# Attention beside a gated feature layer on one core: feature tiles end in pairs, row maxima go bank by bank, and the eight PSUM banks are named by hand

## The chip, the cores and the metric

The kernel runs on one core of a Trainium2 chip. The metric is the device time of one execution in microseconds. The core has five engines with a queue of instructions each: TensorE (PE in the profile, its weight loads PEld), VectorE (DVE), ScalarE (ACT), GpSimd (POOL) and SyncE (SP, which here only issues DMAs). Each queue runs in order; across queues, instructions wait for one another through semaphores. TensorE writes its results to PSUM, which this kernel uses as eight banks of 128 x 512 fp32 values.

## The reference

For one sequence x of S = 2048 tokens and D = 448 features:

```
g   = sigmoid(x . gate_w)                                   one number a token
a   = (softmax(q k^T / sqrt(28)) v) wo                      16 heads of 28 features
b   = (relu(x W_gate) * (x W_up)) W_down                    1792 hidden features
out = g * a + (1 - g) * b
```

All data are fp32. TensorE gets fp32 precision from reduced-precision passes by splitting operands into a high and a low part: a product over the 448 features takes eleven passes (the list TERMS), since the last 64 features of both parts share one pass with another.

## The kernel before, in words

The order of the instructions is written out by hand; no scheduler moves them. The work has three stages.

*The front part* projects x to q, k and v. Units of eleven passes for q and k (`qk`, line 324) alternate with units for v (`vproj`, line 342). From the tenth unit on, row maxima of the first heads and, at the end, the first 16 scores are put between the passes.

*The rounds* are the bulk: 256 pairs of head and key tile (16 heads, 16 tiles of 128 keys), eight tiles a round, 32 rounds. Each character of an order string is one step:

- `s` is one block of scores, 128 keys by 512 queries (`scores`, line 180, TensorE), and its exponential (line 182, ScalarE) into a slot for probabilities. Four blocks make a key tile, 32 a round.
- `m` is a piece of the row maxima that softmax subtracts (`smax`). For 128 queries, TensorE computes the products with the keys (line 152) and VectorE takes the largest (line 154). A head needs 16 x 4 blocks of 128 x 512. Maxima run ahead of the scores by LEAD tiles and more. When a head is finished, `smax_end` transposes its 128 x 16 maxima (line 162), splits them and writes them by DMA as two extra rows of Q, so that the score matmul subtracts them.
- `x` is one pass of the feature layer of b (`gu_mm`, line 489): a half tile is 128 of the gate or of the up features for 512 tokens and takes eleven passes. A finished gate half goes through relu (`relu`, ScalarE, in LATE rounds VectorE), a finished up half is multiplied by it on VectorE and sent to DRAM (`spill_h`, lines 505 and 511).
- `h` ends two half tiles together: their last passes need only 64 rows each, sit in the upper and the lower half of the array, and run side by side. This is called a pair here.
- `l` and `u` are steps of the first round alone: the last store of the front part, and the loads of the third head with the split of the second half of the first weights.

After the string of a round come the splits of the next feature weights (`split_f`: ScalarE the high part, POOL the low part, line 99), then `pv` (line 524): the value product of the eight key tiles, 32 fp32 matmuls, which the trace records as 64, on column tiles of 32, into one bank. It goes to OS by a copy on ScalarE (line 528, first half of a head) or an add on VectorE (line 530, second half).

`FIRST` is the order of the first round, `LONG` has three half tiles in a round, `WIDE` four, and `LATE` is for the last three rounds, which have no maxima.

PSUM comes from three pools of the scheduling layer: `ps_s`, two banks for scores; `ps_x`, two for feature passes and the transpose; `ps_w`, two tiles of two banks each for maxima and value products. The layer chooses which buffer of a pool a new tile gets.

*The rest* after the rounds has five feature tiles (`gate_up`), the down projection (line 741), the output projection (`wout`, line 697) and the mix of both.

The small steps that the prediction speaks of: `row_sums` (line 538) inverts the sums of the probabilities of a head, `spread` broadcasts them by DMA from POOL's queue, `normalise` (line 549) multiplies. SP's queue carries the loads of K and Q of later heads (lines 134 and 139) and of the raw feature weights (`fetch_f`, line 209), in the order in which they are issued. The raw weights of the first tile lie in a buffer called `pair`, whose other half holds the last stored qk tile until its DMA is done; the third Q takes that buffer.

Of the kernel before, what the change touches and what calls it, by code (L numbers as in the profile page):

```python
# [29 lines left out]
NK = S // P  # L30
SCALE = DH ** -0.5
# [36 lines left out]
def gated_mix_kernel(ctx, tc, x, wq, wo, wgu, wd, out):  # L68
# [11 lines left out]
    def ps_s(name):  # L80
        return psum.tile([P, TB], F32, tag="s", bufs=2, name=name)

    def ps_w(name):
        return psum.tile([P, 2, TB], F32, tag="mx", bufs=2, name=name)

    def ps_x(name):
        return psum.tile([P, TB], F32, tag="x", bufs=2, name=name)
# [54 lines left out]
    maxima = [(h, u, half) for h in range(H) for u in range(NK) for half in range(2)]  # L142

    def smax(k):

        h, u, half = maxima[k]
        if u == 0 and half == 0:
            MX[h] = keep.tile([P, 32], F32, name=f"mx_{h}", tag="mx", bufs=2)
        ps = ps_w(f"sm_{k}")
        for c in range(2):  # L150
            k0 = (half * 2 + c) * TB
            nc.tensor.matmul(ps[:, c, :], Q[h][:GD, u * P:(u + 1) * P], K[h % 3][:GD, k0:k0 + TB],  # L152
                             start=True, stop=True)
        nc.vector.tensor_reduce(MX[h][:, 2 * u + half:2 * u + half + 1], ps, axis=AX.XY, op=OP.max)  # L154
        if u == NK - 1 and half == 1:
            M[h] = keep.tile([P, 16], F32, name=f"m_{h}", tag="m", bufs=2)
            nc.vector.tensor_reduce(M[h], MX.pop(h).rearrange("p (a b) -> p a b", b=2), axis=AX.X, op=OP.max)

    def smax_end(h):

        pt = ps_x(f"mt_{h}")
        nc.tensor.transpose(pt[:16, :P], M.pop(h), ident)  # L162
        mh = keep.tile([16, 2, P], F32R, name=f"mh_{h}", tag="mh", bufs=1)
# [7 lines left out]
        return rest  # L171
# [3 lines left out]
    def scores(i, j):  # L175
        h, kt = divmod(i, NK)
        if j == 0:
            PT[i] = p_slot(i % NP, f"P_{i}")
        ps = ps_s(f"s_{i}_{j}")
        nc.tensor.matmul(ps, K[h % 3][:GD + 2, kt * P:(kt + 1) * P], Q[h][:GD + 2, j * TB:(j + 1) * TB],  # L180
                         start=True, stop=True)
        nc.scalar.activation(PT[i][:, j], ps, AF.Exp, scale=SCALE)  # L182

    def scores_pair(i, j):

        h, kt = divmod(i, NK)
        if j == 0:
            PT[i] = p_slot(i % NP, f"P_{i}")
        ps = ps_w(f"s_{i}_{j}")
        for c in range(2):  # L190
            nc.tensor.matmul(ps[:, c], K[h % 3][:GD + 2, kt * P:(kt + 1) * P], Q[h][:GD + 2, (j + c) * TB:(j + c + 1) * TB],  # L191
                             start=True, stop=True)
        nc.scalar.activation(PT[i][:, j:j + 2], ps, AF.Exp, scale=SCALE)
# [18 lines left out]
    with tc.tile_pool(name="qkv", bufs=1) as pa:  # L212
# [82 lines left out]
        turn = [3]  # L295

        def ps_any(name, late=False):
            turn[0] += 1
            return (ps_s, ps_s, ps_x, ps_x)[turn[0] % 4](name) if not late else ps_x(name)
# [21 lines left out]
        def qk(tb, c, terms=TERMS, among=()):  # L321
            ps = ps_any(f"qk_{tb}_{c}", c == NQ - 1)
# [12 lines left out]
            sends.append(send)  # L335
            if (tb, c) != (0, NQ - 1):
                sends.pop()()

        def vproj(tb, t, among=()):
            ps = ps_any(f"v_{tb}_{t}", tb == 0 and t > 1)  # L340
# [26 lines left out]
        ps = ps_x("warm_ps")  # L367
# [49 lines left out]
        m, first, ahead = 0, 9, 2 * LEAD + 4  # L417
        for n, (f, *a) in enumerate(mixed):
# [16 lines left out]
            while n >= first and m < (n + 1 - first) * ahead / (len(mixed) - first):  # L435
                among.append((smax, m))
                m += 1
# [5 lines left out]
            if 0 in M and ends >= 2 * NK:  # L443
                smax_end(0)()
        assert m == ahead, m

    def gates():
# [11 lines left out]
    SECOND = {sum(n for _, n in ROUNDS[:r + 1]) - 1 - 2 * k for r in range(len(ROUNDS))  # L459
              for k in range(ROUNDS[r][0].count("h"))}  # L460
# [53 lines left out]
    NI = H * NK  # L514
    OS, LS = {}, {}

    def pv(i0, ni):

        h = i0 // NK
        po = ps_w(f"po_{i0}")[:, 0]  # L520
# [5 lines left out]
        if i0 % NK == 0:  # L526
            OS[h] = fe.tile([P, TB], F32, name=f"os_{h}", tag="os", bufs=2)
            nc.scalar.activation(OS[h], po, AF.Copy)
        else:
            nc.vector.tensor_tensor(OS[h], po, OS[h], op=OP.add)  # L530
# [62 lines left out]
    wor = None  # L593
    for r, (order, nu) in enumerate(ROUNDS):
# [5 lines left out]
        rest = None  # L600
        if m % (2 * NK) == 0 and i0 <= NI - LEAD:
            rest = smax_end(m // (2 * NK) - 1)
            if late:
                rest()
# [6 lines left out]
        for o in order:  # L611
            if o == "x" and not passes:
                continue
            if o == "s":
                i, j = i0 + 1 + ns // NB, ns % NB
                if ns == 4 * NB:
                    small_things(i0 // 4 + 1)
                if len(EARLY) <= i * NB + j < NI * NB and not late:
                    scores(i, j)
                elif late and i < NI and j % 2 == 0:  # L620
                    scores_pair(i, j)
                ns += 1
            elif o == "m":
                smax(m)
                m += 1

                if rest:
                    rest()
                    rest = None
            elif o == "x":  # L630
                i, half, n = passes.pop(0)
                if n == 0:
                    ps = (ps_s if late and len(units) < 2 else ps_x)(f"gu_{i}_{half}")
                    units.append((i, half, ps))
                gu_mm(units[-1][2], i, half, n)
                if n == NT - 1:
                    i, half, ps = units.pop()
                    spill_h(i, ps) if half else relu(i, ps, late)
# [32 lines left out]
    assert i0 == NI and m == len(maxima), (i0, m)  # L671
# [19 lines left out]

    def wout(tb, t):
        if t % 2 == 0:
            GA[tb, t // 2] = ps_w(f"wo_{tb}_{t}")
        ps = GA[tb, t // 2]
        for n, (a, b) in enumerate(TERMS):
            nc.tensor.matmul(ps[:, t % 2, :D], ON[tb][b // 4][:, b % 4, t * P:(t + 1) * P], WO[:, a], start=(n == 0),  # L697
# [3 lines left out]
        if t % 2:  # L701
            for u in (t - 1, t):
                k = tb * 4 + u
                nc.vector.tensor_scalar(GA[tb][:, u], ps[:, u % 2, :D], gate[:, 0, k:k + 1], None, op0=OP.mult)

    def gate_up(i):
# [8 lines left out]
        relu(i, ps[:, 0])  # L715
        spill_h(i, ps[:, 1])
# [37 lines left out]
    def down(i):  # L754
        tb, f = divmod(i, NF)
        if f == 0:
            ACC[tb] = [ps_s(f"acc_{tb}_0"), ps_s(f"acc_{tb}_1"), ps_x(f"acc_{tb}_2"), ps_x(f"acc_{tb}_3")]
# [82 lines left out]
```

## Time and profile before

| | us |
|---|---|
| median of 3 runs (lowest, highest) | 1289.51 (1289.47, 1290.0) |
| the profiled execution | 1289.54 |
| its span in the profile | 1287.8 |
| TensorE busy | 1281.6 |
| VectorE busy | 809.7 |
| ScalarE busy | 743.2 |
| POOL busy | 365.9 |

A line of a group in the profile reads: line of the kernel, engine, operation, output<-input, shapes, count | busy us, mean ns of one | idle time before it, and what ended that idle time. A line of the timeline reads: start in us, duration, engine, line, operation, names, shapes, count, and in brackets the idle time before it. The durations of matmuls overlap, so the distance between two starts tells what one costs. A line of a stretch gives its bounds and its length, the busy time of PE, PEld, DVE, ACT and POOL with the numbers of their instructions, the granted clock, the busy share of the DMA engines, and GB/s.

### The profile page before, as it was taken

What the parts mean: (1) busy time and instruction counts of PE and PEld (TensorE: products, weight loads), DVE (VectorE), ACT (ScalarE), POOL (GpSimd) and SP (SyncE); (2) the same over time, 40 slices, a digit from 0 to 9 for tenths busy, and PEclk for the clock granted to TensorE, in tenths of its full rate; (3) what the DMA queues carried; (4) which work ended last, traced back from release to release, by engine and by line L of the source; (5) the groups of instructions that cost most, each with busy time, mean ns of one, the idle gap of its engine ahead of it and who ended that gap; (6) DMA issues with size and microseconds to landing.
All of it is one profiled execution on the core that took longest, in us unless ns stands there. A gap on an engine that the chain in (4) does not pass through costs nothing.

```text
span 1287.8 us, 17721 instructions
## 1 busy us (share of the span) xinstructions
PE 1281.6 (100%) x6687; PEld 926.6 (72%) x6687; DVE 809.7 (63%) x839; ACT 743.2 (58%) x1387; POOL 365.9 (28%) x551
## 2 busy tenths in 40 slices
PE   9999999999999999999999999999999999999998
PEld 6888766666666666666666666666666666899997
DVE  6487766667676777777766667777777223663342
ACT  6212766666667667676766666767676765322121
POOL 3222121323223322222223323223232354651020
PEclk9999999999999999999999999999999999999999
DMA  9845523141426233141534142332331224644432
GB/s 319 290 160 232 144 87 91 59 122 48 119 79 180 71 85 96 55 106 43 138 99 124 57 107 77 95 84 73 98 116 41 82 87 152 205 135 144 139 106 78
DMA packets 53566, 148.87 MB, mean 116 GB/s; under 512 B 10025, under 2 KB 17129, under 8 KB 48873
## 3 DMA queue, kind: packets, MB, share of 16 engines
q1 hardware_dynamic: 36120, 98.34, 27.9%
q0 software_dynamic: 16928, 48.93, 10.9%
q8 instruction: 53, 0.87, 0.3%
q10 hardware_dynamic: 432, 0.46, 0.1%
q14 instruction: 33, 0.26, 0.1%
HBM read 102.06 MB, written 46.02 MB: 115 GB/s over the span
## 4 chain that ended last, share of the span: by engine, by line
PE 99%; DVE 0%; ACT 0%; issue 0%
PE gu L489 22%; PE sm L152 19%; PE po L524 17%; PE s L180 17%; PE acc L741 11%; PE qk L324 6%; PE v L342 3%; PE wo L697 3%; PE s L191 2%; PE warm_ps L369 0%; PE mt L162 0%; DVE mx L154 0%; DVE y L747 0%; ACT V L346 0%; DVE warm L366 0%
## 5 line engine op out<-in xcount | busy, mean ns | idle before, releaser
L154 DVE TENSOR_REDUCE mx<-sm 128x1 f32<-128x1024 f32 x512 | 612.8, 1222 | 183.5 <-PE sm L152 183.1
L182 ACT ACTIVATE P<-s 128x512 f32<-128x512 f32 x724 | 401.6, 596 | 175.3 <-PE s L180 166.4
L489 PE MATMUL gu<-X,wg 128*128 128x512 f32 (+1 forms) x1232 | 421.9, 400 | 0.0
L180 PE MATMUL s<-Q,K 114*128 114x512 f32 x932 | 362.6, 396 | 0.0
L152 PE MATMUL sm<-K,Q 112*128 112x512 f32 x1024 | 321.7, 395 | 0.9 <-DVE mx L154 0.9
L489 PEld LDWEIGHTS gu<-X,wg 128*128 128x128 f32 (+1 forms) x1232 | 226.4, 189 | 64.0 <-issue 13.8
L152 PEld LDWEIGHTS sm<-K,Q 112*128 112x128 f32 x1024 | 194.4, 190 | 42.5 <-DVE mx L154 1.7
L180 PEld LDWEIGHTS s<-Q,K 114*128 114x128 f32 x932 | 176.3, 189 | 49.5 <-issue 10.1
L511 POOL DMA_DIRECT2D h_d<-h x56 | 31.5, 563 | 601.1 <-DVE h L505 367.7
L524 PE MATMUL po<-P,V 128*32 128x512 f32 x1600 | 181.0, 594 | 0.0
L99 POOL TENSOR_TENSOR wg<-wgr,wg 128x384 fp32r<-128x384 f32 x204 | 145.9, 733 | 8.1
L182 ACT ACTIVATE V<-s 128x512 f32<-128x512 f32 x208 | 115.1, 596 | 46.2 <-PE s L180 44.3
L741 PE MATMUL acc<-WD,hh 128*128 128x448 f32 x672 | 140.9, 368 | 0.0
L741 PEld LDWEIGHTS acc<-WD,hh 128*128 128x128 f32 x672 | 126.1, 188 | 12.9
L524 PEld LDWEIGHTS po<-P,V 128*32 128x32 f32 x1600 | 49.5, 110 | 111.5 <-issue 106.8
L90 ACT ACTIVATE hh<-hr 128x512 fp32r<-128x512 f32 x56 | 35.2, 631 | 118.9 <-PE acc L741 118.9
L96 DVE TENSOR_TENSOR hh<-hr,hh 128x512 fp32r<-128x512 f32 x56 | 46.1, 824 | 64.2 <-ACT hh L90 64.2
L324 PE MATMUL qk<-X,W 128*128 128x512 f32 x308 | 79.2, 399 | 0.1
L324 PEld LDWEIGHTS qk<-X,W 128*128 128x128 f32 x308 | 58.2, 190 | 14.8 <-DVE X L96 1.0
L90 ACT ACTIVATE wg<-wgr 128x384 fp32r<-128x384 f32 x165 | 66.3, 490 | 4.0 <-DMA wgr<-wgu 2.8
L530 DVE TENSOR_TENSOR os<-po,os 128x512 f32<-128x512 f32 x16 | 11.1, 692 | 79.3 <-PE po L524 79.3
L505 DVE TENSOR_TENSOR h<-gu,rl 128x512 f32<-128x512 f32 x56 | 38.7, 692 | 28.0 <-ACT rl L502 23.0
(72 smaller groups left out, 720.4 us busy)
## 6 DMA issues: line engine op xcount, KB each, us to landing
wgr<-wgu SPq DMA_DIRECT2D x55, 512.0 KB
K<-qk_d SPq DMA_DIRECT2D x64, 224.0 KB
Q<-qk_d SPq DMA_DIRECT2D x64, 224.0 KB
h_d<-h POOLq DMA_DIRECT2D x56, 256.0 KB, 2.4
hr<-h_d SPq DMA_DIRECT2D x56, 256.0 KB
qk_d<-st POOLq DMA_DIRECT2D x21, 512.0 KB, 3.8
x_d<-X POOLq DMA_DIRECT2D x6, 1024.0 KB, 5.1
X<-x_d SPq DMA_DIRECT2D x24, 256.0 KB
```

The lines of the kernel that those rows point to most:

```text
L90: nc.scalar.activation(dst, src, AF.Copy)
L96: nc.vector.tensor_tensor(dst, src, f32(high), op=OP.subtract)
L99: nc.gpsimd.tensor_tensor(dst, src, f32(high), op=OP.subtract)
L152: nc.tensor.matmul(ps[:, c, :], Q[h][:GD, u * P:(u + 1) * P], K[h % 3][:GD, k0:k0 + TB], start=True, stop=True)
L154: nc.vector.tensor_reduce(MX[h][:, 2 * u + half:2 * u + half + 1], ps, axis=AX.XY, op=OP.max)
L180: nc.tensor.matmul(ps, K[h % 3][:GD + 2, kt * P:(kt + 1) * P], Q[h][:GD + 2, j * TB:(j + 1) * TB], start=True, stop=True)
L182: nc.scalar.activation(PT[i][:, j], ps, AF.Exp, scale=SCALE)
L324: nc.tensor.matmul(ps, W[:, a, c * P:(c + 1) * P], xf(tb, b), start=(n == 0), stop=(n == NT - 1))
L489: nc.tensor.matmul(ps, WS[i][rows, s, a], xf(i // NF, b)[rows], start=(n == 0), stop=(n == NT - 1))
L505: nc.vector.tensor_tensor(h, ps, RL.pop(i), op=OP.mult)
L524: nc.tensor.matmul(po[32 * j:32 * j + 32], V[:, h // 4 % 2, i % NK, h % 4], p[:, j], start=(i == i0), stop=(i == i0 + ni - 1))
L741: nc.tensor.matmul(ACC[i // NF][t][:, :D], HH[i][:, a, t * P:(t + 1) * P], WD[:, f, b], start=(f == 0 and n == 0), stop=(f == NF - 1 and n ...
```

## The change

- Every half tile from the second round on makes only ten passes in the string, and its last pass comes in a pair. A LONG round has 30 `x` instead of 31. LONG rounds come in twos: the first ends with one pair (`h`) and carries its third half tile, ten passes done, into the second, which ends with two pairs (`hh`). WIDE has 40 `x` and two pairs instead of 42 and one. LATE keeps 40 and two.
- A maximum `m` is now one block, one bank and one reduction of 512 instead of two blocks, two banks and one reduction of 1024. LONG and WIDE have 32 `m` instead of 16, the first round 16 instead of 12, the front part 112 blocks instead of 104. In LONG the order is score, maximum, pass, over and over.
- The pools go. Eight banks are named, and each kind of work takes its banks in turn: scores 0 and 1; feature passes 4 to 7, up to four half tiles open at once; maxima and value products 2 and 3, with one maximum a round in a feature bank that is still free, and 2, 3, 6, 7 in the front part and the first round; LATE scores and value products 0 to 3.
- Scores were a key tile ahead of the round's own tiles (`i0 + 1`) and are not any more; the slots for probabilities go from 9 to 8. The first round has 16 scores instead of 20, the last one 32 instead of 28.
- LATE scores come one bank at a time, where two banks had one exponential.
- The copy of OS moves from ScalarE to VectorE. The transposed maxima are first copied out of PSUM by ScalarE, and split after the third score, the low part by POOL instead of VectorE.
- After the rounds the same steps use pairs of the named banks.

```diff
-FIRST = "s" * 12 + "mmlssxxxmsxsxuxmsxmsxsxmsxsxmsxsxmsxsxmsxsxmsxsxmsxsxmsx"
-LONG = "smsxmsxsxmsxsxmsxsmxsxsmxsxsxmsxsmxsxsxxxsmsmsxxsxmsxsxmsxsmxsxsmxsxsxmsxsmxxssh"
-WIDE = "xssmxxsxxsxxmssxmxsxxmssmxxsxsmxsxsmxsxsxxxxxxssmxxsxxmsxsmxsxsmxsxmsxsmxsxsmxsxxsmsxxsmxsh"
-LATE = "ssxxxssxxxssxxssxx" * 4 + "hh"
-ROUNDS = [(FIRST, 2)] + ([(LONG, 3)] * 2 + [(WIDE, 4)]) * 2 + [(LONG, 3)] * 2
-ROUNDS += ([(WIDE, 4)] + [(LONG, 3)] * 8) * 2 + [(LONG, 3)] * 2 + [(LATE, 4)] * 3
-NP = 9
+FIRST = "ssssssssssssssssmmmmlssxxxsxxxsxummsxsxxmmxsxsmmxxsxsmmxsxsxmmsxsxxmmssx"
+LONG = "smsmxsmmsxxsmxsmxsmxsmxsmxsmxsmxsmxsmxsmxsmxsmxsmxsmxsmxsmxsmxsmxsmxsmxsmxsmxsmxsmxsmxsmxsmxsm"
+WIDE = "smsmxsmmsxxsmxsmxsmxxsmxsmxsmxxsmxsmxsmxxsmxsmxsmxxsmxsmxxsmxsmxsmxxsmxsmxsmxxsmxsmxsmxxsmxsmxsmxxsmxsmxhh"
+LATE = "sxsxsxsxx" * 8 + "hh"
+TWO = [(LONG + "h", 3), (LONG + "hh", 3)]
+ROUNDS = [(FIRST, 2)] + (TWO + [(WIDE, 4)]) * 2 + TWO
+ROUNDS += ([(WIDE, 4)] + TWO * 4) * 2 + TWO + [(LATE, 4)] * 3
+NP = 8
...
+    banks = [psum.tile([P, TB], F32, name=f"b_{k}") for k in range(8)]
+    def turn(kind, among):
+        count[kind] = count.get(kind, -1) + 1
+        return among[count[kind] % len(among)]
+    def ps_s():
+        return banks[turn("s", (0, 1))]
+    def ps_w():
+        return banks[turn("w", (2, 3, 6, 7))]
+    def ps_m():
+        return banks[turn("m", (3, 2))]
+    def ps_p():
+        return banks[turn("p", (0, 1, 2, 3))]
+    def ps_f():
+        return banks[turn("f", (4, 5, 6, 7))]
+    def later(n):
+        return banks[4 + (count["f"] + 1 + n) % 4]
...
-        for c in range(2):
-            k0 = (half * 2 + c) * TB
-            nc.tensor.matmul(ps[:, c, :], Q[h][:GD, u * P:(u + 1) * P], K[h % 3][:GD, k0:k0 + TB],
-                             start=True, stop=True)
-        nc.vector.tensor_reduce(MX[h][:, 2 * u + half:2 * u + half + 1], ps, axis=AX.XY, op=OP.max)
+        nc.tensor.matmul(ps, Q[h][:GD, u * P:(u + 1) * P], K[h % 3][:GD, c * TB:(c + 1) * TB], start=True, stop=True)
+        nc.vector.tensor_reduce(MX[h][:, 4 * u + c:4 * u + c + 1], ps, axis=AX.X, op=OP.max)
...
-        act_high(mh[:, 0], pt[:16, :P])
-        def rest():
-            low(mh[:, 1], pt[:16, :P], mh[:, 0])
+        def parts():
+            act_high(mh[:, 0], mr)
+            pool_low(mh[:, 1], mr, mh[:, 0])
             for r in range(2):
                 nc.gpsimd.dma_start(f32(Q[h])[GD + r:GD + r + 1], f32(mh)[:, r])
+        return [lambda: nc.scalar.activation(mr, pt[:16, :P], AF.Copy), parts]
...
-        ps = ps_s(f"s_{i}_{j}")
+        ps = ps_s() if i < NI - 3 * NK // 2 else ps_p()
...
-        m, first, ahead = 0, 9, 2 * LEAD + 4
+        m, first, ahead = 0, 9, 4 * LEAD + 16
...
-        po = ps_w(f"po_{i0}")[:, 0]
+        po = ps_w() if i0 == 0 else ps_m() if i0 < NI - 3 * NK // 2 else ps_p()
...
-            nc.scalar.activation(OS[h], po, AF.Copy)
+            nc.vector.tensor_copy(OS[h], po)
...
-        passes = [(*divmod(k, 2), n) for k in todo for n in range(NT - (k >= nxt - 2 * order.count("h")))]
-        units = []
+        passes = [(*divmod(k, 2), n) for k in todo for n in range(NT - (r > 0))]
...
-                i, j = i0 + 1 + ns // NB, ns % NB
+                i, j = i0 + ns // NB, ns % NB
...
+                if rest and ns in (1, 3):
+                    rest.pop(0)()
...
-                smax(m)
+                smax(m, ps_w() if r == 0 else later(1) if order[:n].count("m") == 1 else ps_m())
...
+    def ps_two():
+        two = turn("two", ((2, 3), (6, 7)))
+        return turn("two", ((2, 3), (6, 7))) if two in held else two
...
-        ps = ps_w(f"gu_{i}")
+        ps = [banks[k] for k in ps_two()]
         for s in range(2):
             for n in range(NT):
-                gu_mm(ps[:, s], i, s, n)
+                gu_mm(ps[s], i, s, n)
```

More of the change, by code (lines that the diff above doesn't have):

```diff
@@ L78, in f32, with ps_x @@
         return ap.bitcast(F32)
[L80 to L87, printed above, removed]
+    banks = [psum.tile([P, TB], F32, name=f"b_{k}") for k in range(8)]
+    count = {}
+    def turn(kind, among):
[3 more added lines that the diff above has]
+        return banks[turn("s", (0, 1))]
+    def ps_x():
+        return banks[turn("x", (4, 5))]
+    def ps_w():
[8 more added lines that the diff above has]
+        return banks[4 + (count["f"] + 1 + n) % 4]
     def act_high(dst, src):
@@ L141, in gated_mix_kernel, with smax, smax_end @@
     MX, M = {}, {}
[L142 to L149, printed above, removed]
[L150 to L155 removed]
+    def smax(k, ps):
+        h, u, c = k // (4 * NK), k // 4 % NK, k % 4
+        if u == 0 and c == 0:
+            MX[h] = keep.tile([P, 64], F32, name=f"mx_{h}", tag="mx", bufs=2)
+        nc.tensor.matmul(ps, Q[h][:GD, u * P:(u + 1) * P], K[h % 3][:GD, c * TB:(c + 1) * TB], start=True, stop=True)
+        nc.vector.tensor_reduce(MX[h][:, 4 * u + c:4 * u + c + 1], ps, axis=AX.X, op=OP.max)
+        if u == NK - 1 and c == 3:
             M[h] = keep.tile([P, 16], F32, name=f"m_{h}", tag="m", bufs=2)
[L157 to L161 removed]
+            nc.vector.tensor_reduce(M[h], MX.pop(h).rearrange("p (a b) -> p a b", b=4), axis=AX.X, op=OP.max)
+    def smax_end(h, pt):
         nc.tensor.transpose(pt[:16, :P], M.pop(h), ident)
+        mr = keep.tile([16, P], F32, name=f"mr_{h}", tag="mr", bufs=1)
         mh = keep.tile([16, 2, P], F32R, name=f"mh_{h}", tag="mh", bufs=1)
[L164 to L167 removed]
+        def parts():
+            act_high(mh[:, 0], mr)
+            pool_low(mh[:, 1], mr, mh[:, 0])
             for r in range(2):
                 nc.gpsimd.dma_start(f32(Q[h])[GD + r:GD + r + 1], f32(mh)[:, r])
[L171 removed]
+        return [lambda: nc.scalar.activation(mr, pt[:16, :P], AF.Copy), parts]
     PT = {}
@@ L182, in scores @@
         nc.scalar.activation(PT[i][:, j], ps, AF.Exp, scale=SCALE)
[L184 to L193, printed above, removed]
     X = {}
@@ L293, in spill_x, with ps_any @@
             nc.gpsimd.dma_start(x_d[tb, r], f32(X[tb][r]))
[L295 to L299, printed above, removed]
+        def ps_any(late=False):
+            return (ps_x if late else turn("any", (ps_s, ps_s, ps_x, ps_x)))()
         def mix(n, among):
@@ L339, in vproj @@
         def vproj(tb, t, among=()):
-            ps = ps_any(f"v_{tb}_{t}", tb == 0 and t > 1)
+            ps = ps_any(tb == 0 and t > 1)
             for n, (a, b) in enumerate(TERMS):
@@ L441, in gated_mix_kernel @@
             f(*a, among=among)
-            if 0 in M and ends >= 2 * NK:
-                smax_end(0)()
+            if 0 in M and ends >= 4 * NK:
+                for part in smax_end(0, ps_x()):
+                    part()
         assert m == ahead, m
@@ L458, in gated_mix_kernel @@
     done = sum(n for _, n in ROUNDS) // 2
-    SECOND = {sum(n for _, n in ROUNDS[:r + 1]) - 1 - 2 * k for r in range(len(ROUNDS))
-              for k in range(ROUNDS[r][0].count("h"))}
+    SECOND = set(range(ROUNDS[0][1] + 1, 2 * done, 2))
     def lane(k):
@@ L599, in gated_mix_kernel @@
         small_things(i0 // 4)
[L600 to L604, printed above, removed]
+        rest = []
+        if m % (4 * NK) == 0 and i0 <= NI - LEAD:
+            rest = smax_end(m // (4 * NK) - 1, later(2))
+            while late and rest:
+                rest.pop(0)()
         if late and wor is None:
             wor = load_wo()
-        passes = [(*divmod(k, 2), n) for k in todo for n in range(NT - (k >= nxt - 2 * order.count("h")))]
-        units = []
+        passes = [(*divmod(k, 2), n) for k in todo for n in range(NT - (r > 0))]
         ns = 0
-        for o in order:
-            if o == "x" and not passes:
-                continue
+        for n, o in enumerate(order):
             if o == "s":
-                i, j = i0 + 1 + ns // NB, ns % NB
+                i, j = i0 + ns // NB, ns % NB
                 if ns == 4 * NB:
                     small_things(i0 // 4 + 1)
-                if len(EARLY) <= i * NB + j < NI * NB and not late:
+                if len(EARLY) <= i * NB + j:
                     scores(i, j)
-                elif late and i < NI and j % 2 == 0:
-                    scores_pair(i, j)
                 ns += 1
+                if rest and ns in (1, 3):
+                    rest.pop(0)()
             elif o == "m":
-                smax(m)
+                smax(m, ps_w() if r == 0 else later(1) if order[:n].count("m") == 1 else ps_m())
                 m += 1
-                if rest:
-                    rest()
-                    rest = None
             elif o == "x":
[L631 to L636, printed above, removed]
+                i, half, k = passes.pop(0)
+                if k == 0:
+                    units.append((i, half, ps_f()))
+                gu_mm(units[-1][2], i, half, k)
+                if k == NT - 1:
                     i, half, ps = units.pop()
@@ L670, in gated_mix_kernel @@
             split_wo(wor)
-    assert i0 == NI and m == len(maxima), (i0, m)
+    assert i0 == NI and m == 4 * NK * H and not units, (i0, m)
     stk.close()
@@ L690, in split_o @@
         pool_low(ON[tb][1][:, c], OR[tb][:, c], ON[tb][0][:, c])
+    held = []
+    def ps_two():
+        two = turn("two", ((2, 3), (6, 7)))
+        return turn("two", ((2, 3), (6, 7))) if two in held else two
     def wout(tb, t):
         if t % 2 == 0:
-            GA[tb, t // 2] = ps_w(f"wo_{tb}_{t}")
-        ps = GA[tb, t // 2]
+            held.append(ps_two())
+        ps = banks[held[0][t % 2]]
         for n, (a, b) in enumerate(TERMS):
-            nc.tensor.matmul(ps[:, t % 2, :D], ON[tb][b // 4][:, b % 4, t * P:(t + 1) * P], WO[:, a], start=(n == 0),
+            nc.tensor.matmul(ps[:, :D], ON[tb][b // 4][:, b % 4, t * P:(t + 1) * P], WO[:, a], start=(n == 0),
                              stop=(n == NT - 1))
@@ L703, in wout @@
                 k = tb * 4 + u
-                nc.vector.tensor_scalar(GA[tb][:, u], ps[:, u % 2, :D], gate[:, 0, k:k + 1], None, op0=OP.mult)
+                nc.vector.tensor_scalar(GA[tb][:, u], banks[held[0][u % 2]][:, :D], gate[:, 0, k:k + 1], None, op0=OP.mult)
+            held.pop()
     def gate_up(i):
@@ L756, in down @@
         if f == 0:
-            ACC[tb] = [ps_s(f"acc_{tb}_0"), ps_s(f"acc_{tb}_1"), ps_x(f"acc_{tb}_2"), ps_x(f"acc_{tb}_3")]
+            ACC[tb] = [banks[k] for k in (0, 1, 4, 5)]
         if i not in LAST:
```

14 lines of the change are left out of this document (7 added, 7 removed).

## The prediction

> **What bounds the kernel now.** I read the page first (engines, slices, chain of waits), then sums by stretch for single rounds, then the timeline around the places where a round begins and ends.
>
> ```profile
> span 1287.8 us, 17721 instructions
> ...
> PE 1281.6 (100%) x6687; PEld 926.6 (72%) x6687; DVE 809.7 (63%) x839; ACT 743.2 (58%) x1387; POOL 365.9 (28%) x551
> ...
> PE 99%; DVE 0%; ACT 0%; issue 0%
> ```
> Three stretches: length, then busy time of TensorE, its weight loads, VectorE, ScalarE and POOL, then the clock.
> ```profile
> 523.93:553.67 29.74, 29.74 (x164) 20.12 (x163) 20.73 (x22) 19.86 (x39) 7.49 (x13) 1.00 0.14 45
> 1033.80:1058.60 24.80, 24.80 (x148) 15.55 (x140) 6.62 (x8) 18.27 (x22) 9.61 (x16) 1.00 0.23 74
> 53.00:107.00 54.00, 54.00 (x245) 45.88 (x244) 43.54 (x42) 9.65 (x24) 12.05 (x17) 1.00 0.54 205
> ```
> TensorE is never idle, its granted clock is 1.00 in each stretch, and the chain of waits is TensorE for 99%. In one LONG round (first row), one LATE round (second) and the front part (third) it is busy all of the time, with VectorE at 20.7 of 29.7 us, 6.6 of 24.8 and 43.5 of 54. So a change gains only by taking issue slots from TensorE, and loses only where TensorE has to wait. The profiled execution took 1289.54 us, 1.74 beside its span; it stands 0.03 above the median 1289.51. 0.2% is 2.58 us, about what a measurement here can tell from no change.
>
> **What a slot and a pair cost.** Starts of matmuls in the timeline give the slots (the durations overlap):
>
> ```profile
> 1095.97 5.15 PE gu L489 x22
> ...
> 158.19 0.40 PE L180 MATMUL s<-Q,K 114*128 114x512 f32 x1
> 158.43 0.39 PE L489 MATMUL gu<-X,wg 128*128 128x512 f32 x1
> 158.75 1.50 PE L524 MATMUL po<-P,V 128*32 128x512 f32 x12
> ...
> 553.11 0.63 PE L180 MATMUL s<-Q,K 114*128 114x512 f32 x2
> 553.67 0.50 PE L489 MATMUL gu<-X,wg 64*128 64x512 f32 x2
> 554.10 1.92 PE L524 MATMUL po<-V 128*32 128x512 f32 x16
> ...
> 1026.05 1.30 PE L489 MATMUL gu<-X,wg 128*128 128x512 f32 x6
> 1027.28 1.07 PE L524 MATMUL po<-P,V 128*32 128x512 f32 x8
> ```
> A plain matmul is 5.15/22 = 0.233 us. Two plain matmuls and then the value product (po) take 158.19 to 158.75 = 0.56; two plain and one pair of 64-row matmuls 553.11 to 554.10 = 0.99; two plain and two pairs (the six of 1026.05) 1.23. So the first pair costs 0.43 for two matmuls that would take 0.47: nearly nothing is gained. The second costs 0.24 and saves 0.466 - 0.24 = 0.226.
>
> **The change on TensorE.** Pairs go from 34 (24 LONG and 4 WIDE rounds with one, 3 LATE with two) to 50 (12 LONG with one, 12 with two, 4 WIDE and 3 LATE with two). All 16 new ones are second pairs: 16 x 0.226 = 3.6 us off the path. Bounds: 16 x 0.04 = 0.6, if a second pair cost what a first does, to 3.7, a whole slot each; I take 3.6, since the LATE row is the same matmul in the same place. Scores, maxima, transposes and value products keep their number. Scores one key tile later and maxima earlier only move slots: the front part gets 112 banks for 104 (8 x 0.233 = 1.86 us more), the first round loses 4 scores and 8 banks (2.8 less), the last LATE round gets 4 scores.
>
> **The change on VectorE.** 512 reductions of two banks become 1024 of one.
>
> ```profile
> L154 DVE TENSOR_REDUCE mx<-sm 128x1 f32<-128x1024 f32 x512 | 612.8, 1222 | 183.5 <-PE sm L152 183.1
> ...
> L530 DVE TENSOR_TENSOR os<-po,os 128x512 f32<-128x512 f32 x16 | 11.1, 692 | 79.3 <-PE po L524 79.3
> ...
> L538 DVE RECIPROCAL rs<-ls 128x16 f32<-128x16 f32 x16 | 3.9, 244 | 0.2 <-DMA ls<-os 0.2
> ...
> 555.15 0.69 DVE L505 TENSOR_TENSOR h<-gu,rl 128x512 f32<-128x512 f32 x1 [1.07 <-ACT rl L502]
> 555.75 0.68 DVE L549 TENSOR_TENSOR os<-os,rb 128x512 f32<-128x512 f32 x1
> ```
> And the start of a round, without a transpose, with one, and the one where TensorE waited:
> ```profile
> 561.10 0.50 PE L180 MATMUL s<-Q,K 114*128 114x512 f32 x1
> 561.24 0.69 DVE L530 TENSOR_TENSOR os<-po,os 128x512 f32<-128x512 f32 x1 [4.80 <-PE po L524]
> 561.44 0.64 PE L152 MATMUL sm<-K,Q 112*128 112x512 f32 x2
> 562.12 2.35 DVE L154 TENSOR_REDUCE mx<-sm 128x1 f32<-128x1024 f32 x2 [0.18 <-PE sm L152]
> ...
> 531.40 0.48 PE L180 MATMUL s<-Q,K 114*128 114x512 f32 x1
> 531.51 0.60 ACT L528 ACTIVATE os<-po 128x512 f32<-128x512 f32 x1 [5.00 <-PE po L524]
> 531.72 0.64 PE L152 MATMUL sm<-K,Q 112*128 112x512 f32 x2
> ...
> 166.78 1.23 DVE L154 TENSOR_REDUCE mx<-sm 128x1 f32<-128x1024 f32 x1 [6.23 <-PE sm L152]
> 168.06 0.73 PE L152 MATMUL sm<-K,Q 112*128 112x512 f32 x2 [0.86 <-DVE mx L154]
> ```
> A one-bank reduction is not in the trace. Half the long one is 0.61, another 512-wide operation on one bank 0.69; I take 0.69, the same width, and 0.61 as the spacing when they follow each other, as 555.15 and 555.75 do. The new LONG order is score, maximum, pass: one maximum every 3 slots = 0.70 us, so VectorE has 0.09 to spare each. Two banks alternate, so a bank must be back in 1.40: matmul 0.40, start 0.04 (561.44 + 0.64 to 562.12), reduction 0.69, wake 0.05 (166.78 + 1.23 to 168.06), 1.18 in all. Per round VectorE gets 32 x 0.69 = 22.1 for 16 x 1.22 = 19.6, and the products with relu now come only at the round's end, beside the 7.0 us of value products (554.10 to 561.10). In the front part a unit of qk and one of v hold 9 maxima (9 x 0.61 + 0.69 = 6.2 us) in 6.9 of TensorE, with four banks.
>
> The tight place is the start of a round. From its first score T (561.10), os starts at 0.14, the first maximum is issued at 0.34 and reduced from 0.78, the second from 1.39, the third from 2.00 to 2.69; its bank is asked for again in slot 13, T + 0.34 + 11 x 0.233 = 2.90: 0.16 to spare. In the 14 rounds with a transpose (531.40) the copy of os, now VectorE's, starts at 0.11 and a reciprocal follows, so the third ends by 2.87, slot 13 is at 2.88: nothing to spare, nothing lost. Each 0.1 us more on VectorE there costs 28 x 0.1.
>
> ScalarE loses that copy and gets one of 16 rows, inside its 10 us of slack per round. In LATE, single exponentials replace pairs: 32 of 0.60 (the width of 531.51) are 19.2 of 24.8 us, the splits fit beside the value products, and four banks stand in front: no cost. The reciprocal now stands behind the copy of os on VectorE, so the broadcasts on POOL's queue start after the value product instead of beside it, and behind them the low part of the maxima (new on POOL) and their two DMAs. All are wanted at the end of that round or in the next, 20 us later: no cost. The ninth slot for probabilities goes; the first exponential of a round overwrites what the value product read first, 7 us earlier: no wait.
>
> **Waits that go and come.**
>
> ```profile
> 154.74 1.59 SPq L139 DMA_DIRECT2D Q<-qk_d  x4
> 163.15 1.24 ACT L90 ACTIVATE wg<-wgr 128x384 fp32r<-128x384 f32 x3 [2.80 <-DMA wgr<-wgu]
> 165.79 0.48 PE L180 MATMUL s<-Q,K 114*128 114x512 f32 x1
> ...
> 1082.92 1.44 PE L489 MATMUL gu<-X,wg 128*128 128x512 f32 x5
> 1083.13 0.69 DVE L530 TENSOR_TENSOR os<-po,os 128x512 f32<-128x512 f32 x1 [3.89 <-PE po L524]
> ```
> Second round: the 0.86 us that TensorE waited at 168.06, for a maximum that got the buffer of the one before it, goes, as the banks now alternate by hand. But SP's Q load waits for the store of the front part's last qk tile, whose buffer it takes; it and the weight fetch queued behind it move 1.86 later, while the first score comes 0.93 earlier (164.86). ScalarE waits in order for that fetch until 165.0, splits for 1.24, and starts the first exponential at 166.24; the third score wants its bank at 166.1 and gets it 0.60 + 0.05 later, at 166.9: 0.8 lost (bounds 0 and 1.6). Net -0.1.
> End of the rounds: the last value product now lies in the bank that the next gate matmul writes (counting turns over four banks: the 99th is bank 2). That matmul, free at 1082.92 before, waits for os to 1083.13 + 0.69 + 0.05 = 1083.87, and all of TensorE's in-order queue behind it: +0.95 (bounds 0.8 and 1.0).
> Sum: 1289.54 - 3.6 - 0.1 + 0.95 = 1286.8, as for the median.
>
> **Rivals.**
> *ScalarE is not late in the second round* (fetch lands sooner): 0.8 less, 1286.0. For it, a fetch of 0.5 MB alone need not take long; against it, the Q load is in front of it on the queue.
>
> *VectorE gives banks back late.* If one-bank reductions follow each other in 0.69, not 0.61, slot 13 is late by 0.05 in 14 rounds and 0.28 in 14: +4.6, 1291.4. The row of 555.75 speaks against it. The Trainium skill, "VectorE: DVE Perf Modes", section "The DRAIN you can't avoid", says that the next operation does not start until the pipe is empty, and that only one which is not held starts earlier. By the first half of it this case comes out; the trace here shows 0.60 between starts for a duration of 0.69.
>
> *VectorE's copy of os waits for POOL* (the slower one).
>
> ```profile
> 560.68 1.96 POOL L99 TENSOR_TENSOR wg<-wgr,wg 128x384 fp32r<-128x384 f32 x3
> 1143.46 1.60 POOL L99 TENSOR_TENSOR WD<-wdr,WD 128x448 fp32r<-128x448 f32 x1
> 1143.98 1.33 DVE L93 CAST WD<-wdr 128x448 fp32r<-128x448 f32 x1
> ```
> A VectorE cast beside a POOL operation took 1.33 us, and POOL is at work where a round begins. Then the first reduction of those 14 rounds ends 0.63 too late for slot 8: +8.8, 1295.6. From 0.38 a round on it is slower. Against it: this copy reads PSUM. The Trainium skill, "SBUF — State Buffer", section "Who interferes with whom", says that an instruction with at most one SBUF input, outside the two-port modes, does not contend with GpSimd; by that rule this case falls away. No copy from PSUM beside POOL is in this trace.
>
> *VectorE is the bound:* a one-bank reduction above 0.70, say 0.72: 32 x 0.02 x 28 rounds = 18 us, 1305. Against it are both rows above.
>
> *The change does not do what it says:* a second pair in a LONG round costs 0.43: 0.6 saved, 1289.8.
>
> **Chances.** Forecast 0.52 (1286.1 to 1287.6, a little over half of it below 1286.93, the 0.2% line); ScalarE on time 0.14; banks late 0.12; copy waits 0.09; VectorE bound 0.07; pairs save nothing 0.06. Faster 0.29 + 0.14 = 0.43; within 0.2% 0.23 + 0.12 + 0.06 = 0.41; slower 0.16. Range 1285.6 to 1291.5: it leaves out the two slower cases.
>
> **What would show it.** In the changed profile: 100 matmuls of 64 rows for 68; LONG rounds in turn 0.23 shorter and equal, WIDE 0.23 shorter; one-bank reductions of 0.69 with VectorE waiting for TensorE between them; TensorE idle only near 166 (waiting for ScalarE) and once, 0.95, after the last value product. I am wrong if TensorE waits for VectorE in each round, most of all in its fifth or fourth maximum, or if os copies last over 1 us.

## The result, and the profile after

The changed kernel takes 1291.28 us (median of 22 runs, 1290.83 to 1292.33), the kernel before 1289.47 on the same chips; the ratio is 1.0015 with a 95% interval of 1.0008 to 1.0021. The forecast was 1286.8. It is slower, by about 1.8 us.

From the page of the kernel after: the span, the busy times, the chain of waits by engine, and two groups.

```profile
span 1289.5 us, 18247 instructions
...
PE 1281.9 (99%) x6687; PEld 919.7 (71%) x6687; DVE 899.5 (70%) x1351; ACT 780.4 (61%) x1433; POOL 372.7 (29%) x567
...
PE 99%; DMA 0%; DVE 0%; issue 0%; ACT 0%; POOL 0%; DVEq 0%; ACTq 0%; POOLq 0%
...
L176 DVE TENSOR_REDUCE mx<-b 128x1 f32<-128x512 f32 x1024 | 696.1, 689 | 31.4 <-PE b L175 21.9
...
L535 DVE COPY os<-b 128x512 f32<-128x512 f32 x16 | 11.1, 692 | 87.8 <-PE b L531 87.8
```

TensorE is busy as long as before (1281.9 for 1281.6), although it has 16 slots less to issue. The one-bank reduction takes the 0.69 of the forecast, and the copy of OS is not slowed. The wait of 0.9 for VectorE in the second round is gone. Beside one of 0.2 in the front part, two of TensorE's waits are new (engine and line, what it waited for, us in total, times, longest):

```profile
PE b L497 <- POOL wg L126: 1.1, 1, 1.1
PE b L497 <- DVE os L537: 1.0, 1, 1.0
```

The second is the wait behind the rounds, forecast at 0.95. The first is in the first round and was not forecast. Where the rest went is seen when the span is cut at the starts of the value products:

| | before | forecast | after |
|---|---|---|---|
| start to the first value product | 158.75 | -0.93 | +0.43 |
| to the second | 30.90 | -0.29 | -1.36 |
| to the 29th, 27 rounds with maxima | 812.82 | -3.4 | +0.66 |
| to the 32nd, LATE rounds | 73.44 | +0.93 | +0.97 |
| to the last matmul | 207.46 | +0.95 | +1.00 |

The first two rows and the last two come out together near their forecast (1.0 for 0.7). The miss of 4.1 lies in the 27 rounds, and in each of them alike. Two LONG rounds, with two pairs and with one (the first number behind the bounds is the length):

```profile
523.43:553.34 29.91, 29.91 (x166) 19.90 (x164) 23.71 (x37) 21.14 (x40) 7.39 (x13) 1.00 0.11 37
553.34:582.97 29.63, 29.63 (x162) 19.76 (x160) 24.13 (x37) 22.21 (x40) 9.56 (x15) 1.00 0.48 124
```

Forecast were 29.72 or 29.73 and 29.49. The second pair costs what was said (29.91 - 29.63 = 0.28 here, 0.25 in the mean of all LONG rounds, for 0.24), but every round is about 0.15 too long, and TensorE shows no wait in it. Half of the 0.15 is at the start of a round. From the timeline there, with the weight loads:

```profile
560.34 0.50 PE L202 MATMUL b<-Q,K 114*128 114x512 f32 x1
...
560.94 1.08 ACT L204 ACTIVATE P<-b 128x512 f32<-128x512 f32 x2 [4.40 <-PE b L202]
...
561.39 0.40 PE L497 MATMUL b<-X,wg 128*128 128x512 f32 x1
561.59 0.19 PEld L202 LDWEIGHTS b<-Q,K 114*128 114x128 f32 x1 [0.24 <-ACT P L204]
561.63 0.46 PE L202 MATMUL b<-Q,K 114*128 114x512 f32 x1
...
561.93 0.40 PE L175 MATMUL b<-K,Q 112*128 112x512 f32 x1
```

The third score of the round is its sixth matmul now; before it was the eighth. Its bank is that of the first score, which ScalarE reads from 560.94 on, for 0.60. The wait sits on the weight load, which otherwise starts together with the matmul before it (here at 561.39). It starts at 561.59, and the next matmul starts 0.30 behind the score, not 0.23. Of the two fences that follow, the first is the row of the weight loads' waits of the kernel after that shows this for all rounds, the second the same wait before. The us in these rows are idle time of the weight loads; of each wait the matmuls lose 0.07 to 0.09:

```profile
PEld b L202 <- ACT P L204: 7.1, 29, 0.4
```
```profile
PEld s L180 <- ACT P L182: 0.4, 2, 0.2
```

The other half is spread over all slots. Two scores far apart in a LONG round, before and then after:

```profile
563.31 0.39 PE L180 MATMUL s<-Q,K 114*128 114x512 f32 x1
...
581.66 0.39 PE L180 MATMUL s<-Q,K 114*128 114x512 f32 x1
```
```profile
563.09 0.39 PE L202 MATMUL b<-Q,K 114*128 114x512 f32 x1
...
581.99 0.40 PE L202 MATMUL b<-Q,K 114*128 114x512 f32 x1
```

Before, 79 slots in 18.35 us are 0.2323 each; after, 27 times score, maximum, pass, 81 slots in 18.90, are 0.2333. From the 13th slot on, the mean over the 27 rounds differs by 0.0008; with some 82 slots a round that is 1.9 us. The first twelve slots, the one behind the third score above all, are 0.09 longer a round, which makes another 2.4: together about the 4.1. Why a slot is longer is what most of the experiments are about.

### The profile page after: what moved, and what is told of

Same layout as the page of the kernel before. It is cut to its first block, busy times and chain, and to the rows that moved or that the text cites. A ratio compares the mean times of both kernels' runs of the same rounds, so it can differ in the third digit from the quotient of the medians.

```text
span 1289.5 us, 18247 instructions
## 1 busy us (share of the span) xinstructions
PE 1281.9 (99%) x6687; PEld 919.7 (71%) x6687; DVE 899.5 (70%) x1351; ACT 780.4 (61%) x1433; POOL 372.7 (29%) x567
## 4 chain that ended last, share of the span: by engine, by line
PE 99%; DMA 0%; DVE 0%; issue 0%; ACT 0%; POOL 0%; DVEq 0%; ACTq 0%; POOLq 0%
PE b L497 22%; PE b L202 19%; PE b L175 19%; PE b L531 17%; PE b L749 11%; PE b L332 5%; PE b L350 3%; PE b L704 3%; DMA wr<-wq 0%; PE b L183 0%; DVE W L123 0%; DVE X L123 0%; POOL wg L126 0%; DVE os L537 0%; DVE y L755 0%
## 5 line engine op out<-in xcount | busy, mean ns | idle before, releaser
L176 DVE TENSOR_REDUCE mx<-b 128x1 f32<-128x512 f32 x1024 | 696.1, 689 | 31.4 <-PE b L175 21.9
L204 ACT ACTIVATE P<-b 128x512 f32<-128x512 f32 x768 | 450.3, 598 | 223.9 <-PE b L202 165.6
L497 PE MATMUL b<-X,wg 128*128 128x512 f32 (+1 forms) x1232 | 434.6, 400 | 2.1 <-POOL wg L126 1.1
L202 PE MATMUL b<-Q,K 114*128 114x512 f32 x1024 | 410.3, 401 | 0.0
L175 PE MATMUL b<-K,Q 112*128 112x512 f32 x1024 | 399.1, 396 | 0.0
L497 PEld LDWEIGHTS b<-X,wg 128*128 128x128 f32 (+1 forms) x1232 | 222.8, 190 | 58.5 <-issue 13.0
L202 PEld LDWEIGHTS b<-Q,K 114*128 114x128 f32 x1024 | 194.4, 190 | 63.0 <-issue 13.4
L175 PEld LDWEIGHTS b<-K,Q 112*128 112x128 f32 x1024 | 192.3, 188 | 47.8 <-issue 0.2
L531 PE MATMUL b<-P,V 128*32 128x512 f32 x1536 | 177.3, 594 | 0.0
L204 ACT ACTIVATE V<-b 128x512 f32<-128x512 f32 x256 | 150.7, 598 | 26.4 <-PE b L202 4.3
```

The costliest lines, as they stand in the source:

```text
L175: nc.tensor.matmul(ps, Q[h][:GD, u * P:(u + 1) * P], K[h % 3][:GD, c * TB:(c + 1) * TB], start=True, stop=True)
L176: nc.vector.tensor_reduce(MX[h][:, 4 * u + c:4 * u + c + 1], ps, axis=AX.X, op=OP.max)
L497: nc.tensor.matmul(ps, WS[i][rows, s, a], xf(i // NF, b)[rows], start=(n == 0), stop=(n == NT - 1))
L531: nc.tensor.matmul(po[32 * j:32 * j + 32], V[:, h // 4 % 2, i % NK, h % 4], p[:, j], start=(i == i0), stop=(i == i0 + ni - 1))
```

## The experiments

In a slot, the weight load takes 0.19 and the matmul starts some 0.04 behind its end. My first theory was drawn from the trace: 624 of the 648 weight loads for maxima in the even part of the rounds start 0.052 to 0.055 us behind the end of the reduction that gives their bank back. From matmul to reduction 0.43, reduction 0.69, 0.05, and 0.22 that the weight load is ahead of its matmul make 1.40, and two banks are wanted in 1.395.

**Trading the third score and the third maximum.**

```diff
-LONG = "smsmxsmmsxx...
+LONG = "smsmxmsmsxx...
```


> Only the third score and the third maximum of a round trade places. In the changed kernel the slot behind the third score takes 0.30 to 0.32 us for 0.23, in every round with maxima. Theory (banks asked for by the weight load, one slot ahead of the matmul): the third score's weight load waits for its bank, which ScalarE's first exponential gives back; a slot later it no longer waits, but then the fifth maximum, which gets the bank of the third, is asked for 0.09 before VectorE has read it, and waits instead. So almost nothing is gained: 1290.8 to 1291.3, with the long slot now in front of the fifth maximum. Rival (ScalarE's bank is the only late thing at the start of a round): 28 x 0.08 = 2.2 us off, 1289.0, and no long slot is left there.

Measured: 1290.37 (1289.66 to 1291.0), 0.9 less than the changed kernel. The long slot is gone from its place. A wait of another score's weight load comes later in the round:

```profile
562.49 0.19 PEld L202 LDWEIGHTS b<-Q,K 114*128 114x128 f32 x1 [0.18 <-ACT P L204]
```

The slot behind it takes 0.25, and the other slots are a little longer than in the changed kernel. Neither theory had that: the wait does not go to VectorE's bank but to a later score, so ScalarE, not only one of its banks, is late at the start of a round. Less than half of the 2.2 comes back.

**A third bank for the maxima, and shorter reductions.** Two ways to take the late bank away.

```diff
     def ps_m():
-        return banks[turn("m", (3, 2))]
+        around.append(around.pop(0))
+        return banks[around[-1]]
...
+        if r and "m" in order:
+            third = later(len(todo) - bool(units)) if len(todo) == 3 else later(3)
+            around.insert(1, third)
...
+            if third in around and len(passes) <= keep_for:
+                around.remove(third)
```


> The maxima get a third bank, one that the gate tiles do not yet need: for a whole round with one pair, until some three passes ahead of the last tile in the others. Theory (two banks are short: matmul to reduction 0.43, reduction 0.69, wake 0.05 and the weight load 0.22 ahead make 1.40 of 1.395): a plain slot in those stretches goes back from 0.2334 to 0.2324 us, some 2120 slots x 0.0009 = 1.9 us off, 1289.4; the weight load of a maximum no longer starts 0.05 behind a reduction's end; the long slot at the third score stays. Rival (a matmul that waits and signals by itself has a longer slot, whatever bank it writes): slots stay at 0.2334, 1291.3.

```diff
-        nc.vector.tensor_reduce(MX[h][...], ps, axis=AX.X, op=OP.max)
+        nc.vector.tensor_reduce(MX[h][...], ps[:, :448], axis=AX.X, op=OP.max)
```


> The reductions of the maxima leave out the last 64 columns of each bank (so the maxima are those of 448 of every 512 keys); banks, waits and signals stay as they are. Theory (the bank comes back late by some ns): a reduction of 0.625 for 0.692 makes the cycle 1.335, under 1.395; all plain slots return to 0.2324, 28 x 91 x 0.0009 = 2.3 us off, 1289.0. The wait at the third score stays, as it is ScalarE's. Rival (signals lengthen the slot): 1291.3 and 0.2334.

Measured: 1291.58 (1291.4 to 1291.98) and 1291.96 (1291.58 to 1293.54): nothing gained. In the run with short reductions the weight loads of the maxima start 0.003 behind the matmul before them, all of them, so none waits; a slot is as long as it was. Its reductions, and two scores 81 slots apart:

```profile
L176 DVE TENSOR_REDUCE mx<-b 128x1 f32<-128x448 f32 x1024 | 630.6, 622 | 95.1 <-PE b L175 37.5
```
```profile
563.67 0.40 PE L202 MATMUL b<-Q,K 114*128 114x512 f32 x1
...
582.57 0.40 PE L202 MATMUL b<-Q,K 114*128 114x512 f32 x1
```

18.90 us again, 0.2333. The theory of the late bank falls. The bank does come back at the last moment in the changed kernel, but the slot would be 0.2333 without that: the two happen to agree within some ns.

**All edits together.** The traded start, the third bank, banks 6 and 7 first behind the rounds, and a first round in which the split and its maxima are placed otherwise.

```diff
-        two = turn("two", ((2, 3), (6, 7)))
+        two = turn("two", ((6, 7), (2, 3)))
...
-FIRST = "ssssssssssssssssmmmmlssxxxsxxxsxummsxsxxmmxsxsmmxxsxsmmxsxsxmmsxsxxmmssx"
+FIRST = "ssssssssssssssssmmlssmmxxxsxxxusxmmsxsmmxmmxsxxsmmxsxsxmmxsxsxmmsxsxssxx"
```


> Third score and third maximum traded, the third bank, the first tile pair behind the rounds in banks 6 and 7 and not in 2 and 3, and a first round in which two maxima move behind the first scores, the second half of the split is a score earlier and four maxima stand ahead of the tenth pass. Theory: the slots 1.9 off, the long slot at the third score 28 x 0.08 = 2.2 off (the fifth maximum now gets the bank of the second and does not wait), 1.0 off behind the rounds, 1.1 to 1.3 off in the first round: 1285.1, faster than the kernel before by some 4.4. Rival (only the named waits of the profile, at the first round and behind the rounds, are waits; the slots are what they are): 1289.1.

Measured: 1288.41 (1288.23 to 1290.9), ratio to the kernel before 0.9994, 0.9985 to 1.0004. TensorE's waits of this run, which holds neither of the two new ones:

```profile
PE b L379 <- DVE warm L376: 1.2, 1, 1.2
PE b L334 <- DVE X L125: 0.4, 1, 0.4
```

The two waits and the little of the traded start are 2.9 us; the slots stayed at 0.2334. That is the rival's side (1289.1).

**The turn of the matmuls.** What was left was the order itself. The changed kernel repeats score, maximum, pass; the order before has maxima and passes mostly in twos. Both runs are the run with all edits, with other strings:

```diff
-LONG = "smsmxmsmsxx" + "smx" * 27 + "sm"
+LONG = "smsmxmsmsxx" + "sxm" * 27 + "sm"
```


> The run with all four edits, and from the twelfth slot of a round on the cycle score, pass, maximum for score, maximum, pass (the same matmuls, in the other turn). Theory (a slot depends on which matmul follows which): the kernel before has 0.2307 from a score to a pass, 0.2318 from a pass to a maximum and 0.2301 from a maximum to a score, 0.2309 in the mean, where the cycle score, maximum, pass has 0.2335; 28 rounds x some 80 slots x 0.0026 = 5.8 us off that run's 1288.4, 1282.6. Rival (a longer slot is followed by a shorter one, and the mean is that of one signal and one wait for each matmul): 0.2334 as there, 1288.4.

```diff
-LONG = "smsmxmsmsxx" + "smx" * 27 + "sm"
+LONG = "smsmxmsmsxx" + "smmsxx" * 7 + "smx" * 13 + "sm"
```


> The run with all four edits, and in the LONG rounds seven times score, two maxima, score, two passes where score, maximum, pass stood fourteen times, while the third bank is there; as in the kernel before, maxima in twos and passes in twos. Theory (a slot depends on which matmul follows which): these 42 slots take 0.2325 as in the kernel before, not 0.2335; 24 rounds x 42 x 0.001 = 1.0 off, 1287.4. Rival (the mean is that of the waits and signals, one for each maximum now): 0.2335 there, 1288.4.

Measured: 1291.27 (1290.95 to 1291.51) for the other turn of the three, with slots of 0.2335. So a slot is not a sum of prices of who follows whom: these prices, read from the order before, gave 0.2309. The 2.9 that this run takes more than the run with all edits are for the most part not in these slots. Its LONG string ends `sxmsm`: the last maximum stands two slots behind the one before, not three, and its weight load waits for VectorE. The step from it to the pair takes 0.42 or 0.43 for 0.32 or 0.33, 2.4 us in 24 LONG rounds. And 1286.84 (1286.43 to 1288.01) with twos, ratio 0.998, 0.997 to 0.999: 1.6 less than the run with all edits, where 1.0 was expected, with the same matmuls and one wait and one signal for each maximum in both.

**Twos wherever the third bank is.**

```diff
+ONE = "smmsxx" * 15 + "smms"
+BOTH = "smmsxx" * 9 + "smmsx" + "smx" * 11 + "sm"
+WIDE = "smmsxxx" * 9 + "smmsx" + "smx" * 12 + "hh"
+LATE = "ssxxssxxx" * 8 + "hh"
+TWO = [(ONE + "h", 3), (BOTH + "hh", 3)]
```


> The cycle score, two maxima, score, two passes wherever a third bank for the maxima is there: the whole LONG round with one pair, nine and a half cycles in the one with two, with three passes at a time in WIDE; scores and passes in twos in LATE; the third bank stays to the end of a round with one pair. Theory (the turn of the matmuls sets the slot: 0.2310 in that cycle in the run before, 0.2333 in score, maximum, pass): against that run another 48 slots in each of 12 rounds, 12 in each of 12 and 67 in each of 4 at 0.0023 less, 2.3 us, and up to 0.3 in LATE: 1284.2. Rival (the gain of that run came from its rounds being otherwise different, or a wait at the changed start of a round eats it): 1286.8 or more.

Measured: 1284.13 (1283.74 to 1284.37), ratio 0.9959, 0.9945 to 0.9972. A LONG round with one pair, 29.63 in the changed kernel:

```profile
550.43:579.79 29.36, 29.36 (x163) 19.86 (x161) 22.72 (x37) 22.14 (x40) 9.61 (x15) 1.00 0.47 125
```

WIDE, with passes in threes, kept 0.2333 a slot.

**The pairs alone, taken back.** The changed kernel with one pair a round, as before.

```diff
-TWO = [(LONG + "h", 3), (LONG + "hh", 3)]
+TWO = [(LONG + "xh", 3), (LONG + "xh", 3)]
...
-        passes = [(*divmod(k, 2), n) for k in todo for n in range(NT - (r > 0))]
+        passes = [(*divmod(k, 2), n) for k in todo for n in range(NT - (k in SECOND or k + 1 in SECOND))]
```


> The changed kernel with the pairs of the kernel before: one in each round with maxima, and the other two halves of tiles end with a plain pass each (16 pairs less, 32 plain passes more). If a second pair saves 2 x 0.233 - 0.24 = 0.226 us as forecast, 16 x 0.226 = 3.6 us more, 1294.9. Rival (the change's missing gain is that second pairs save nothing in these rounds): 1291.3 to 1291.9.

Measured: 1300.61 (1300.18 to 1300.72), 9.3 more and not 3.6. A LONG round of each kind:

```profile
527.51:557.79 30.28, 30.16 (x165) 19.90 (x163) 23.88 (x38) 21.17 (x39) 7.99 (x14) 1.00 0.14 45
557.79:587.65 29.86, 29.86 (x164) 19.98 (x162) 23.78 (x36) 22.10 (x40) 8.97 (x14) 1.00 0.44 114
```

The second kind has one pass more than with the pairs (29.86 for 29.63, 0.23). The first should cost the same as with two pairs, 29.91, as a pass takes the place of the second pair; it takes 0.4 more. There a half tile now ends in the middle of the round:

```profile
483.28 0.68 DVE L516 TENSOR_TENSOR h<-b,rl 128x512 f32<-128x512 f32 x1
...
484.61 0.19 PEld L175 LDWEIGHTS b<-K,Q 112*128 112x128 f32 x1 [0.55 <-DVE mx L176]
484.61 0.50 PE L175 MATMUL b<-K,Q 112*128 112x512 f32 x1
```

One product with relu between the maxima makes the next ones late, as VectorE has only 0.7 us for each. So the 3.6 are there, and 12 x 0.4 beside some in WIDE make the rest: in this order of one-bank maxima a half tile that ends inside the string costs more than its pass.

**What about twos saves.** The run with twos once more, with even numbers in WIDE and LATE; and the same kernel whose rounds with one pair take a cycle of six with no two alike in a row.

```diff
-ONE = "smmsxx" * 15 + "smms"
+ONE = "smxsxm" * 15 + "smms"
```


> The run with twos throughout, but the twelve LONG rounds with one pair take score, maximum, pass, score, pass, maximum fifteen times: an even cycle of six in which nothing stands twice in a row. Third bank as there; WIDE and LATE also changed, as in the run beside this one. Theory (a kind that stands twice in a row is what saves): these rounds go back to 0.2333 a slot, 29.57 for 29.37, 12 x 0.2 = 2.4 more than the run beside it. Rival (what costs is a cycle of an odd length, three or seven): they stay at 0.2311 and 29.37.

```diff
-WIDE = "smmsxxx" * 9 + "smmsx" + "smx" * 12 + "hh"
-LATE = "ssxxssxxx" * 8 + "hh"
+WIDE = ("smmsxxxx" + "smmsxx") * 4 + "smmsxx" * 2 + "smx" * 12 + "hh"
+LATE = "ssxxssxxssxxssxxxx" * 4 + "hh"
```


> The run with twos throughout; in WIDE, cycles with two and four passes in turn for those with three, and in LATE scores in twos with two or four passes for two and three. In that run the WIDE rounds had kept 0.2335 a slot and LATE 0.2346. Theory (a cycle in which all stand in even numbers has 0.2311): some 66 slots in each of 4 WIDE rounds at 0.0024 less, 0.6, and 70 in each of 3 LATE rounds at up to 0.0035 less, 0.7: 1282.8. Rival (the slot of these two has to do with the work beside them, not with the turn): 1284.1.

Measured: 1286.59 (1285.97 to 1287.1) and 1283.27 (1283.2 to 1283.48), 3.3 apart where 2.4 was expected, the latter with a ratio of 0.9951, 0.9938 to 0.9965, to the kernel before. Two scores 84 slots apart, without twos, and then with them:

```profile
559.11 0.40 PE L205 MATMUL b<-Q,K 114*128 114x512 f32 x1
...
578.71 0.40 PE L205 MATMUL b<-Q,K 114*128 114x512 f32 x1
```
```profile
558.38 0.39 PE L205 MATMUL b<-Q,K 114*128 114x512 f32 x1
...
577.79 0.39 PE L205 MATMUL b<-Q,K 114*128 114x512 f32 x1
```

19.60 us, 0.2333, and 19.41 us, 0.2311. An even cycle without repeats is as long as the cycle of three, so the length of the cycle is not it; in WIDE the step from three passes to two and four took a round from 32.16 to 32.21 down to 32.04 to 32.06. LATE gained 0.04 a round, 0.13 in all where up to 0.7 was expected: its slot went from 0.2348 to 0.2342, though scores and passes now stand in even numbers there too. So twos do not give 0.2311 everywhere. This last kernel is the best of the study, 6.2 us faster than the one before.

## Why the prediction was wrong

*A slot is 0.233 wherever it stands.* This is the step that failed. The prediction said that scores later and maxima earlier "only move slots", and priced a slot by one row. The order of the slots is itself a price: 0.2323 in the order before, 0.2333 in the new one, 0.2311 with twos. In the changed kernel that is some 1.9 us, half of what the pairs save. What shows it is one order changed alone: 0.2311 and 0.2333 with the same matmuls in the same rounds.

*ScalarE has slack, so the start of a round is VectorE's matter.* This failed too. The prediction looked at the busy time of ScalarE and followed only the banks of the maxima. The scores have two banks, and the third score came two slots nearer to the first. It also took a bank as wanted when the matmul starts, where the wait is on the weight load, a slot earlier. Cost 2.2 in the changed kernel; trading two steps brought 0.9 back. What the rest needs was not tried.

*Pairs.* Right: 16 second pairs for 0.24 to 0.25 each.

*VectorE.* Right in its sizes: 0.69 a reduction, 0.69 for the copy of OS, and no bound. Two reductions take 1.28 or 1.29 in the rows of the trace, 0.60 apart, so the rival of reductions back to back is out. The Trainium skill, "VectorE: DVE Perf Modes", section "The DRAIN you can't avoid", has the next operation wait for an empty pipe unless it is not held; here even those with waits start 0.08 ahead of the end before them. The rival of a copy slowed by POOL is out as well: 11 of the 16 copies ran beside a subtraction on POOL and took 0.69 like the other five, as "SBUF — State Buffer", section "Who interferes with whom", of the Trainium skill had it.

*The second round.* The wait for ScalarE did not come, as in the first rival: the fetch of the weights came 0.7 later and not 1.9, and the first score 0.4 later and not 0.9 earlier, because the front part and the first round had lost 1.4 against the forecast by then, 1.1 of it in the wait for POOL. That loss was missed: the store and the split for the first tile now stand behind more reductions on VectorE's and POOL's queues, and its tenth pass comes sooner.

*Behind the rounds.* Right: 1.0 for 0.95, and gone with two other banks.

*Banks late*, the rival at 1291.4, names nearly the time measured, but its mechanism is not what happened: with no maximum's bank late, the time was the same.

## What to carry to other kernels

Where TensorE is busy all the time, measure the slot in the new order before pricing what the change saves: 2500 slots by 1 ns are 2.5 us. Follow each bank to the weight load that asks for it, for every engine that gives banks back, not only for the one with the most work. And when a wait seems to explain a length, remove it without moving anything else: here the wait was real and explained nothing.

## What was not expected of the hardware

The slot of a matmul of 512 columns with a weight load of its own depends on the turn of the matmuls: 0.2311 with maxima and passes in twos, 0.2331 to 0.2341 in four orders else (both turns of three, a cycle of six without repeats, and three passes beside two maxima). In LATE, which has no maxima, it is 0.2342 with scores and passes in twos, so this is no rule for twos in general. The Trainium skill, "TensorE: Matmul & The Clock Gate", section "Back-to-back issue gap", says that in a stream of weight loads and matmuls both set the spacing; the trace agrees so far as the matmul starts some 0.04 behind the end of its weight load. Both pieces are a little shorter in twos: in the two stretches of 84 slots the load takes 0.1891 for 0.1905, and the matmul starts 0.0394 behind its end for 0.0400. Why the order matters is open. Banks and the length of the reductions were varied without effect. The signals of the matmuls are not the cause either, as far as the traces show it. In the run with even numbers the first of two passes in a row sends no signal of its own in 183 cycles of six, and in 73 every matmul sends one: both take 1.387 us. The WIDE rounds with passes in threes send fewer and kept 0.2333, and the 22 passes of the prediction's row, with one signal among them, are at 0.234.
